# Seven part products for eight in the first sums of the second block's gate and up projections, and attention in two halves of each chunk's tokens

## The chip, the cores and the metric

The kernel runs on one core of a Trainium2 chip. The metric is the device time of one launch in microseconds (us), the median of several runs; less is better.

The core's engines work at once and wait for one another through semaphores: TensorE (PE) multiplies a stationary 128x128 tile of weights, loaded beforehand (PEld), with a moving tile of up to 512 columns and adds the result into a bank of PSUM; VectorE (DVE) and ScalarE (ACT) do elementwise work on SBUF and PSUM; GpSimd (POOL) and SyncE (SP) mainly issue DMA transfers here.

## What is computed

One transformer block over 2048 tokens of width 1024, with all inputs in bf16:

```python
xn = layernorm(x)
q, k, v = split(xn @ wqkv)                 # 32 heads of 32
# each token attends to itself and 7 earlier ones, 2 apart:
logits[s, w] = q[s] . k[s - 2 * w] * 32 ** -0.5      # -1e9 where s - 2 * w < 0
o = sum_w softmax(logits)[s, w] * v[s - 2 * w]
s = o @ wo
g = silu((silu(xn @ w1) * (xn @ w3)) @ w2)  # w1, w3: 1024 x 3584, w2: 3584 x 1024
out = x + s * g
```

## The kernel before

**Tiling.** Two blocks of 1024 tokens, each of two chunks of 512 tokens: chunks 0 and 1, then 2 and 3. Activations lie transposed in SBUF (`xT`: feature on the partitions, tokens along them; its two halves are the two chunks of a block). A block goes through q, k and v, the gate and up projections (14 steps, `up_step(b, fb)`, 256 columns of w1 and w3 each), the down projection (`mlp_down`) and the output projection of attention (`wo`). Attention of a chunk (`attention(c)`) is VectorE work that lies beside those matmuls.

**Seven products for eight.** Each big product is cut into two by two blocks, and 7 block products with sums of blocks take the place of 8 (Strassen's scheme in Winograd's form). In a gate and up step the row blocks are w1 and w3 (so one scheme yields both), and the column blocks the two chunks. The sums of input blocks are made once a block (`xn_sums`, tile `xs`, four sums), the sums of weights once for each of the 14 steps in the first block (`w_sums`: four sums of 128x1024 on VectorE, tile `st`, r8 buffers), stored to `s_dram` and loaded again in the second (`up_load`, 1 MB a step). A step is 56 matmuls of 128x128 by 512 columns: for each i of two tiles of 128 rows, four for each of 7 products. In `up_step` first the gate product `pa` of both i (4 matmuls each), then the product of the first sums, `pe` (`sl(0, i)` by `tx[0]`). Then the tail of the step before is emitted (`flush`), ScalarE copies `pa` to `pb` (`fork`) and `pe` to an SBUF buffer (`us5`), and the other products add on in those banks, with copies, additions (`ua2`, `uh`) and silu on ScalarE and VectorE between them.

The down projection already has one of its products cut once more in this way (`part` in `mlp_down`, L1070): matmuls of 256 columns into quarters of PSUM banks, ScalarE copies between quarters (`dq21`, `dq5`, `dq2`) and VectorE additions (`dq12`, `dq22`). On VectorE the first of `dq22` is the correction that a following part product of the first block adds to.

**Attention of a chunk.** For each of 8 offsets w: two products of q with shifted k (128x2048 each, one for each half of the 8 feature tiles), an addition of the two (2048), two more that halve (1024, 512), the last into `E`. Four DMAs gather `E` into `L`, so that a head's four parts lie side by side; three additions, a maximum over w, subtraction, exponent (ScalarE, L756), sum, reciprocal and product follow, all in 128x1024 f32 or less; four DMAs spread the weights back into `E`. Then for each half of the feature tiles eight products of `E` with shifted v (2048) are added up into `qo`, which `wo` reads.

**What sets the order.** The program is written as a list of operations with what they read and write (`Plan`). TensorE keeps the list's order. For the other engines a planner inside the kernel gives each operation a due time, worked back from TensorE, and lets each engine take the most urgent that is ready, by fixed costs for each kind; the order that comes out is what each engine then runs, strictly one after another. SP's queue issues the loads and half of the gathers, POOL's queue the stores to `s_dram` and `t_dram` and the other half. Load buffers (`r8`) are six of 1 MB; SBUF for attention (`att`) is three of 512 KB; `k2` are eight buffers of 128x512 f32; PSUM has eight banks (`mm`).

All matmuls of `mm(...)` bear line L356, VectorE's two-operand operations L365 (`tt`), ScalarE's copies L370 (`cp`), silu L373, DMAs L379.

Of the kernel before, what the change touches and what calls it, by code (L numbers as in the profile page):

```python
# [244 lines left out]
def kernel(  # L245
# [44 lines left out]
    t_dram = dram.tile([P, FH, 4, CH], FP16, name="t_dram")  # L290
    park = {k: dram.tile([P, NJ, CH], BF16, name=f"park_{k[0]}{k[1]}")
# [10 lines left out]
    E = const.tile([P, NST, W, P], BF16, name="E")  # L302
# [34 lines left out]
    zero = E[:, 0, 0:4, :].rearrange("p w n -> p (w n)")  # L337
# [56 lines left out]
    def xs_cells(i):  # L394
        return [("xs", i, k) for k in range(KH)]
# [305 lines left out]
    def attention(c):  # L701
        u = c % 2
        J4 = [range(0, 4), range(4, 8)]
        r4 = lambda s: s.ap().rearrange("p (j n) -> p j n", j=4)
# [5 lines left out]
        for w in range(W):  # L710
            o = HALO - DIL * w
            pr = []
            for jh in range(2):
                p_t = plan.slot("att", f"p{c}_{w}_{jh}")
                tt(f"qk{c}", mul, lambda p_t=p_t: r4(p_t), lambda jh=jh: qo[:, u, jh * 4:jh * 4 + 4, :],
                   lambda jh=jh, o=o: kT[:, jh * 4:jh * 4 + 4, o:o + CH],
                   qo_cells(u, J4[jh]) + [("k", j) for j in J4[jh]] + ([("k", j, "halo") for j in J4[jh]] if w else []),
                   [p_t], 2048, True)
                pr.append(p_t)
            p0, p1 = pr  # L720
            tt(f"qa{c}", add, lambda p0=p0: r4(p0), lambda p0=p0: r4(p0), lambda p1=p1: r4(p1), [p0, p1], [p0], 2048, True)
            tt(f"qb{c}", add, lambda p0=p0: r4(p0)[:, 0:2], lambda p0=p0: r4(p0)[:, 0:2], lambda p0=p0: r4(p0)[:, 2:4],
               [p0], [p0], 1024, True)
            tt(f"qc{c}", add, lambda w=w: E[:, :, w, :], lambda p0=p0: r4(p0)[:, 0].rearrange("p (q n) -> p q n", n=P),
               lambda p0=p0: r4(p0)[:, 1].rearrange("p (q n) -> p q n", n=P),
               [p0], [("E", w, sq) for sq in range(4)], 512, True)
        if ("v", c) in park:
            halo("v")
            get(c, "v")
        if c == 0:  # L730
            tt("mask", add, lambda: E[:, 0, :, 0:HALO], lambda: E[:, 0, :, 0:HALO], lambda: maskb[:],
               [("E", w, 0) for w in range(W)], [("E", w, 0) for w in range(W)], 128, False)
        plan.lift = SOFT[c]
        L = plan.slot("att", f"L{c}", 2)
        Lv = lambda r: L.ap().rearrange("p (r w n) -> p r w n", r=NR, w=W)[:, r]
        for sq in range(4):
            dma((POOL, SP)[sq % 2], f"L{c}", lambda sq=sq: L.ap()[sq:P:4].rearrange("h (r n) -> h r n", r=NR),
                lambda sq=sq: E[:, sq].rearrange("p w n -> p (w n)"), [("E", w, sq) for w in range(W)], [(L, sq)], 330, 2048)
        zf = lambda s: s.ap().bitcast(FP32)
        z = plan.slot("att", f"z{c}")  # L740
        zv = lambda: zf(z).rearrange("p (w n) -> p w n", w=W)
        LC = [(L, sq) for sq in range(4)]
        tt(f"z{c}", add, zv, lambda: Lv(0), lambda: Lv(1), LC, [z], 1024, False)
        tt(f"z{c}", add, zv, zv, lambda: Lv(2), LC + [z], [z], 1024, False)
        tt(f"z{c}", add, zv, zv, lambda: Lv(3), LC + [z], [z], 1024, False)
        zm = plan.slot("att", f"zm{c}")
        zt = lambda s: zf(s)[:, 0:512].rearrange("p (w n) -> p w n", w=4)

        def tree(t, op):
            tt(f"tr{c}", op, lambda: zt(t), lambda: zv()[:, 0:4], lambda: zv()[:, 4:8], [z], [t], 512, False)  # L750
            tt(f"tr{c}", op, lambda: zt(t)[:, 0:2], lambda: zt(t)[:, 0:2], lambda: zt(t)[:, 2:4], [t], [t], 256, False)
            tt(f"tr{c}", op, lambda: zt(t)[:, 0:1], lambda: zt(t)[:, 0:1], lambda: zt(t)[:, 1:2], [t], [t], 128, False)

        tree(zm, mx)
        tt(f"zd{c}", sub, zv, zv, lambda: zt(zm)[:, 0:1].to_broadcast([P, W, P]), [z, zm], [z], 1024, False)
        plan.op(ACT, f"exp{c}", lambda: nc.scalar.activation(out=zf(z), in_=zf(z), func=ACTF.Exp, scale=scale),  # L756
                [z], [z], 1.07, 0.11, table="exp")
        zs = plan.slot("att", f"zs{c}")
        tree(zs, add)
        plan.op(DVE, f"rec{c}", lambda: nc.vector.reciprocal(out=zt(zs)[:, 0], in_=zt(zs)[:, 0]), [zs], [zs], 0.87)  # L760
        pb = plan.slot("att", f"pb{c}")
        pbv = lambda: pb.ap()[:, 0:1024].rearrange("p (w n) -> p w n", w=W)
        tt(f"pb{c}", mul, pbv, zv, lambda: zt(zs)[:, 0:1].to_broadcast([P, W, P]), [z, zs], [pb], 1024, False)
        for sq in range(4):
            dma((POOL, SP)[sq % 2], f"E{c}", lambda sq=sq: E[:, sq].rearrange("p w n -> p (w n)"),
                lambda sq=sq: pb.ap()[sq:P:4, 0:1024].unsqueeze(1).to_broadcast([32, NR, 1024]),
                [pb], [("E", w, sq) for w in range(W)], 330, 2048)
        plan.lift = 0.0
        for jh in range(2):
            js = slice(jh * 4, jh * 4 + 4)  # L770
            A = lambda js=js: qo[:, u, js, :]
            Ac = qo_cells(u, J4[jh])

            def pv(dst, wr, w, jh=jh, js=js):
                o = HALO - DIL * w
                q4 = lambda a: a.rearrange("p j (q n) -> p j q n", n=P)
                tt(f"pv{c}", mul, lambda: q4(dst()), lambda: E[:, :, w, :].unsqueeze(1).to_broadcast([P, 4, NST, P]),
                   lambda: q4(vT[:, js, o:o + CH]),
                   [("E", w, sq) for sq in range(4)] + [("v", j) for j in J4[jh]]
                   + ([("v", j, "halo") for j in J4[jh]] if w else []), wr, 2048, True)  # L780

            pv(A, Ac, 0)
            B = plan.slot("att", f"B{c}")
            pv(lambda B=B: r4(B), [B], 1)
            tt(f"pa{c}", add, A, A, lambda B=B: r4(B), Ac + [B], Ac, 2048, True)
            for w0 in (2, 4, 6):
                B, C = plan.slot("att", f"B{c}"), plan.slot("att", f"C{c}")
                pv(lambda B=B: r4(B), [B], w0)
                pv(lambda C=C: r4(C), [C], w0 + 1)
                tt(f"pa{c}", add, lambda B=B: r4(B), lambda B=B: r4(B), lambda C=C: r4(C), [B, C], [B], 2048, True)  # L790
                tt(f"pa{c}", add, A, A, lambda B=B: r4(B), Ac + [B], Ac, 2048, True)

# [11 lines left out]
    def xn_sum4():  # L804
        tt("xs3", sub, lambda: xs[:, 3], lambda: xT[:, 0, KH:KT, :], lambda: xs[:, 1], xt_cells(0, 1) + xs_cells(1), xs_cells(3), 2048, True)

# [10 lines left out]
    def up_load(b, fb):  # L817
# [7 lines left out]
        else:  # L825
            dma(SP, f"st.{fb}", lambda: st_v(st), lambda: s_dram[fb], [("sd", fb)], [(st, q) for q in range(4)], 1024, 8192)
            dma(SP, f"w3.{fb}", lambda: wv()[:, 1, KH:KT], lambda: w3_r[:, KH:KT, fc], [], [(wt, 1, 1)], 256, 512)

    def st_v(st):
        return r8v(st, FP16).rearrange("p (q k n) -> p q k n", q=4, k=KH)  # L830

    def w_sums(fb):
# [8 lines left out]
        tt("ws3", sub, sv(3), wv(0, 1), sv(1), Wc(0, 1) + S_(1), S_(3), 1024, True)  # L841
        dma(POOL, "s_dram", lambda: s_dram[fb], lambda: st_v(st), [(st, q) for q in range(4)], [("sd", fb)], 1024, 8192)

    def up_step(b, fb):
# [15 lines left out]
        for i in I:  # L860
            pa.append(bank(f"ua{b}_{fl[i]}"))
            mm(pa[i], wl(0, 0, i), bx[0, 0], True, [(wt, 0, 0)] + xt_cells(0, 0), mark=[("step", b, fb)])
        for i in I:
            pe.append(bank(f"ue{b}_{fl[i]}"))
            mm(pe[i], sl(0, i), tx[0], True, [(st, 0)] + xs_cells(0))
        flush()
        for i in I:
            pb.append(bank(f"ub{b}_{fl[i]}"))
            cp("fork", pb[i].ap, pa[i].ap, [pa[i]], [pb[i]])
        for i in I:  # L870
            sp5.append(plan.slot("k2", "us5"))
            cp("us5", lambda i=i: f32(sp5[i]), pe[i].ap, [pe[i]], [sp5[i]])
        for i in I:
            mm(pa[i], wl(0, 1, i), bx[0, 1], False, [(wt, 0, 1)] + xt_cells(0, 1))
            silu("hA", hv(i, 0), pa[i].ap, [pa[i]], hc(i, 0), 0.48)
# [472 lines left out]
    for b in range(NB):  # L1348
# [19 lines left out]
        else:  # L1368
# [5 lines left out]
            def second():  # L1374
                xn_sum4()
                wk.extend(qkv_load(1))
# [62 lines left out]
```

## Time and profile before

| What | Before |
|---|---|
| Median of 3 runs | 718.12 us (717.82 to 720.67) |
| Profiled execution, its own time | 718.92 us |
| Its span, first to last instruction | 716.9 us |
| TensorE, matmuls | 706.6 us busy, 99% |
| VectorE | 661.9 us busy, 92% |
| ScalarE | 389.4 us busy, 54% |
| Granted TensorE clock | 0.999 |
| DMA | 150.56 MB, 210 GB/s on average |

The profile is of one execution. "Busy" is time with an instruction of the engine in progress; matmuls follow one another so closely that a busy TensorE says little, and its pace is read from the distance between starts. A group's row gives line, engine, operation, out<-in with shapes, the count, busy time, the mean duration in ns and the idle time before. In the chain of work that ended last, each instruction is followed back to what released it. In a list of stretches, each engine's column is its busy time there, with the count in brackets; then come the granted clock, the DMA share and GB/s.

### The profile page before, as it was taken

The page shows a single profiled execution, that of the slowest core. Times are in us where ns is not written, and L with a number is a line of the kernel's source. Part 1 is how long each engine was busy: PE and PEld are TensorE (multiplying, and loading weights), DVE is VectorE, ACT ScalarE, POOL GpSimd, SP SyncE. Part 2 cuts the span into 40 slices and gives each one's busy share as a digit, 9 for nine tenths or more (in the row PEclk, how much of TensorE's full clock was granted, in tenths as well). Part 3 has the DMA queues.
Part 4 walks back from the last instruction along what each step waited for, and adds up shares of the span by engine and source line. Part 5 has one row for each costly group of instructions (what it writes and reads, how often), then busy time and mean ns, then how long its engine had stood idle before and what let it go on. Part 6 is the DMA issues. An engine that isn't in the chain of part 4 may idle for free.

```text
span 716.9 us, 9340 instructions
## 1 busy us (share of the span) xinstructions
PE 706.6 (99%) x3407; PEld 352.3 (49%) x3462; DVE 661.9 (92%) x901; ACT 389.4 (54%) x668; POOL 25.4 (4%) x54
## 2 busy tenths in 40 slices
PE   8999999999999999999999999999999999999997
PEld 5655544444444444744555554444444444455443
DVE  6999999987999999979799999975999997999968
ACT  6755465567565697534535354657565654422233
POOL 0011100100000000000000000000000000000000
PEclk9999999999999999999999999999999999999999
DMA  8579985866544849695554559897537346437523
GB/s 315 214 247 388 370 295 167 283 207 215 183 169 150 305 127 241 144 299 184 192 156 157 176 183 321 267 307 225 194 109 254 113 157 213 155 128 239 177 73 103
DMA packets 127262, 150.56 MB, mean 210 GB/s; under 512 B 12400, under 2 KB 104176, under 8 KB 122864
## 3 DMA queue, kind: packets, MB, share of 16 engines
q1 hardware_dynamic: 113312, 121.58, 52.3%
q0 software_dynamic: 5312, 26.22, 9.3%
q10 hardware_dynamic: 8592, 2.16, 2.2%
q8 instruction: 27, 0.44, 0.3%
q14 instruction: 19, 0.16, 0.1%
HBM read 106.95 MB, written 32.51 MB: 195 GB/s over the span
## 4 chain that ended last, share of the span: by engine, by line
PE 97%; DVE 1%; DMA 1%; issue 1%; SPq 0%; DVEq 0%
PE mm L356 93%; PE mm L1070 3%; DVE r L365 1%; DMA r<-in_A_wqkv_dram 1%; PE mm L508 0%; SPq L379 0%; DVEq L1434 0%; DVEq L365 0%
## 5 line engine op out<-in xcount | busy, mean ns | idle before, releaser
L356 PEld LDWEIGHTS <-r 128*128 128x128 f16 (+1 forms) x2288 | 239.9, 107 | 245.8 <-DMA r<-in_A_wqkv_dram 2.3
L356 PE MATMUL mm<-xs,r 128*128 128x512 f16 x1280 | 295.2, 379 | 0.0
L356 PE MATMUL mm<-xT,r 128*128 128x512 bf16 (+1 forms) x968 | 224.4, 369 | 3.4 <-DMA r<-in_A_wqkv_dram 1.3
L370 ACT COPY k<-mm 128x512 f32<-128x512 f32 (+1 forms) x200 | 115.0, 579 | 87.0 <-PE mm L356 73.0
L356 PE MATMUL mm<-r,h_sb 128*128 128x512 bf16 (+1 forms) x694 | 153.7, 379 | 0.5
L365 DVE TENSOR_TENSOR att<-att 128x2048 bf16<-128x2048 bf16 (+4 forms) x132 | 124.0, 950 | 7.2 <-ACT att L756 5.2
L356 PEld LDWEIGHTS <-h_sb 128*128 128x128 f16 (+1 forms) x800 | 78.2, 98 | 93.2
L370 ACT COPY mm<-mm 128x512 f32<-128x512 f32 (+1 forms) x92 | 51.5, 563 | 81.7 <-PE mm L356 69.5
L365 DVE TENSOR_TENSOR att<-qo,kT 128x2048 bf16<-128x2048 bf16 x64 | 76.8, 1215 | 0.0
L365 DVE TENSOR_TENSOR att<-E,vT 128x2048 bf16<-128x2048 bf16 x56 | 66.2, 1216 | 0.0
L365 DVE TENSOR_TENSOR h_sb<-mm,k 128x512 bf16<-128x512 f32 x96 | 62.8, 680 | 0.9 <-PE mm L356 0.3
L365 DVE TENSOR_TENSOR r<-r,r 128x1024 f16<-128x1024 bf16 (+6 forms) x76 | 58.9, 784 | 1.9 <-DMA r<-in_A_wqkv_dram 1.3
L373 ACT ACTIVATE k<-k 128x512 bf16<-128x512 f32 x56 | 34.7, 630 | 45.1 <-DVE k L365 45.0
L365 DVE TENSOR_TENSOR k<-mm,k 128x512 f32<-128x512 f32 x72 | 47.8, 683 | 9.8 <-PE mm L356 9.5
L365 DVE TENSOR_TENSOR h_sb<-h_sb,k 128x1024 bf16<-128x1024 bf16 x56 | 37.0, 683 | 14.0 <-ACT k L370 14.0
L373 ACT ACTIVATE h_sb<-mm 128x512 bf16<-128x512 f32 x60 | 35.8, 598 | 18.1 <-PE mm L356 18.0
L370 ACT CAST k<-mm 128x512 bf16<-128x512 f32 x56 | 32.5, 587 | 12.4 <-PE mm L356 12.4
L365 DVE TENSOR_TENSOR qo<-qo,att 128x2048 bf16<-128x2048 bf16 x32 | 38.9, 1215 | 0.0
L365 DVE TENSOR_TENSOR h_sb<-h_sb 128x512 f16<-128x512 bf16 (+1 forms) x72 | 37.4, 561 | 1.0 <-DMA h_sb<-in_B_w_dram 0.8
L365 DVE TENSOR_TENSOR r<-r 128x1024 f16<-128x1024 bf16 (+2 forms) x36 | 27.8, 790 | 0.6 <-DMA r<-t_dram 0.6
L356 PE MATMUL mm<-h_sb 128*128 128x512 f16 x96 | 22.4, 379 | 0.1
L373 ACT ACTIVATE xs<-k 128x512 bf16<-128x512 f32 x8 | 5.0, 630 | 20.6 <-DVE k L365 20.6
(98 smaller groups left out, 378.9 us busy)
## 6 DMA issues: line engine op xcount, KB each, us to landing
r<-in_B_w_dram SPq DMA_DIRECT2D x42, 512.0 KB, 4.0
s_dram<-r POOLq DMA_DIRECT2D x14, 1024.0 KB, 5.5
r<-t_dram SPq DMA_DIRECT2D x16, 896.0 KB, 6.6
r<-s_dram SPq DMA_DIRECT2D x14, 1024.0 KB, 4.9
r<-in_A_wqkv_dram SPq DMA_DIRECT2D x11, 1024.0 KB, 6.8
r<-in_B_w_dram SPq DMA_DIRECT2D x12, 896.0 KB, 4.7
h_sb<-in_B_w_dram SPq DMA_DIRECT2D x14, 512.0 KB, 11.2
t_dram<-h_sb POOLq DMA_DIRECT2D x14, 512.0 KB, 6.9
```

Source lines behind the costliest of these rows:

```text
L356: nc.tensor.matmul(cut(ps.ap()), lhsT=lhs[k](), rhs=cut(rhs[k]()), start=(first and k == 0), stop=(last and k == n - 1), skip_group_check= ...
L365: plan.op(DVE, name, lambda: fn(out=o(), in0=a(), in1=b()), rd, wr, occ, 0.08, late=late)
L370: plan.op(ACT, name, lambda: nc.scalar.copy(out=o(), in_=a()), rd, wr, occ, 0.11)
L373: plan.op(ACT, name, lambda: nc.scalar.activation(out=o(), in_=a(), func=ACTF.Silu), rd, wr, occ, 0.11, table="silu")
L1070: nc.tensor.matmul(ps.ap()[:, col * 256:(col + 1) * 256], lhsT=lhs[k](), rhs=r()[:, k, :], start=first and k == 0, stop=False, skip_group_ ...
```

## The change

*The first sums' product in the second block.* `DEEP` holds for block 1: there the product `pe` of the first sums is itself cut in two by two (the weights' rows by i and its four feature tiles in two pairs; the inputs' 512 columns in two halves), and done as 7 part products of two matmuls of 256 columns each for each step, in place of 8 matmuls of 512. They stand in another order: two parts open the step, ahead of the gate product; the others lie between its later products. Three copies of 256 columns on ScalarE (`uq21`, `uq5`, `uq2`) and two additions of 256 columns on VectorE (`uq12`, `uq22`) join the quarters. The four sums of weights that this needs (128x256 each) are made in `w_sums` in the first block, into the part of the weight tile that held w3's first half, and go through a new `u_dram` (256 KB a step, stored by POOL, loaded by SP between w1 and w3's second half). The four sums of inputs (128x512 each, `xn_sums2`) overwrite a part of `xT`; they are made in both blocks, and read in the second.

*Attention.* Every chunk is worked in two halves of 256 tokens: a product covers all 8 feature tiles for 256 tokens (again 128x2048), and the additions after it have half the size and twice the number (1024, 512, 256). `E` is laid out by halves. Gathers and spreads are 8 DMAs of half the size for 4; softmax is done for each half, in 128x512 f32 or less, so there are two exponents for one. Weighted sums have runs of 64 tokens where there were 128.

```diff
+    u_dram = dram.tile([FB, P, 4 * 2 * P], FP16, name="u_dram")
-    E = const.tile([P, NST, W, P], BF16, name="E")
+    E = const.tile([P, 2, 4, W, CH // 8], BF16, name="E")
...
-            for jh in range(2):
-                p_t = plan.slot("att", f"p{c}_{w}_{jh}")
-                tt(f"qk{c}", mul, ... qo[:, u, jh * 4:jh * 4 + 4, :], ... 2048, True)
-            tt(f"qa{c}", add, ... 2048, True)
-            tt(f"qb{c}", add, ... 1024, True)
-            tt(f"qc{c}", add, lambda w=w: E[:, :, w, :], ... 512, True)
+        for h in H2:
+            for w in range(W):
+                tt(f"qk{c}", mul, pj(0, 8), lambda h=h: qo[:, u, :, tok[h]], kw, qc_(h) + kc, [p], 2048, True)
+                tt(f"qa{c}", add, pj(0, 4), pj(0, 4), pj(4, 8), [p], [p], 1024, True)
+                tt(f"qb{c}", add, pj(0, 2), pj(0, 2), pj(2, 4), [p], [p], 512, True)
+                tt(f"qc{c}", add, lambda w=w, h=h: E[:, h, :, w, :], row(0), row(1), [p], ec(h, [w]), 256, True)
...
+    def xn_sums2():
+        tt("xt0", sub, xv(0), xsq(0, 1), xsq(0, 0), xs_cells(0), xv_cells(0), 512, True)
+        tt("xt2", sub, xv(2), xsq(1, 1), xsq(0, 1), xs_cells(0), xv_cells(2), 512, True)
+        tt("xt1", sub, xv(1), xsq(1, 1), xv(0), xs_cells(0) + xv_cells(0), xv_cells(1), 512, True)
+        tt("xt3", sub, xv(3), xsq(1, 0), xv(1), xs_cells(0) + xv_cells(1), xv_cells(3), 512, True)
...
+            dma(SP, f"su.{fb}", lambda: r8v(wt, FP16)[:, 2048:3072], lambda: u_dram[fb], [("ud", fb)], [(wt, 1, 0)], 256, 2048)
...
+        tt("wu0", add, v(0), a(0, 1), a(1, 1), A, U, 256, True)
+        tt("wu1", sub, v(1), v(0), a(0, 0), A + U, U, 256, True)
+        tt("wu2", sub, v(2), a(0, 0), a(0, 1), A, U, 256, True)
+        tt("wu3", sub, v(3), a(1, 0), v(1), A + U, U, 256, True)
+        dma(POOL, "u_dram", lambda: u_dram[fb], lambda: r8v(wt, FP16)[:, 2048:3072], U, [("ud", fb)], 256, 2048)
...
+    DEEP = lambda b, fb: b == 1
...
+        if DEEP(b, fb):
+            pe = [bank(f"ue{b}_{fl[i]}") for i in I]
+            part(0, 0, sr(0, 0), xr_(0, 0), sc + xc, True)
+            part(0, 1, sw(0), xq(0), wc + xv_cells(0))
+            cp("uq21", h2(pe[1], 0), h2(pe[0], 0), [pe[0]], [pe[1]], 0.3)
+            cp("uq5", h2(hs, 0), h2(pe[0], 1), [pe[0]], [(hs, 0)], 0.3)
+            for i in I:
+                pa.append(bank(f"ua{b}_{fl[i]}"))
+                mm(pa[i], wl(0, 0, i), bx[0, 0], True, [(wt, 0, 0)] + xt_cells(0, 0), mark=[("step", b, fb)])
+            part(0, 0, sr(1, 0), xr_(1, 0), sc + xc)
+            part(1, 0, sw(1), xq(1), wc + xv_cells(1))
+            cp("uq2", h2(hs, 1), h2(pe[1], 0), [pe[1]], [(hs, 1)], 0.3)
+            tt("uq12", add, h2(pe[0], 1), h2(pe[0], 1), h2(hs, 1), [pe[0], (hs, 1)], [pe[0]], 256, False)
+            flush()
...
+            c11(0)
+            part(1, 0, sw(2), ..., wc + xv_cells(2))
+            tt("uq22", add, h2(pe[1], 1), h2(pe[1], 0), h2(hs, 0), [pe[1], (hs, 0)], [pe[1]], 256, False)
+            part(0, 1, sw(3), xr_(1, 1), wc + xc)
+            u5(0)
+            c11(1)
+            u2(0)
+            part(1, 0, sr(1, 1), xq(3), sc + xv_cells(3))
+            u5(1)
+            u2(1)
```

Where `part(i, h, ...)` emits two matmuls of 256 columns into half h of the bank `pe[i]`, `c11(i)` is the gate product's second part, `u2(i)` the product of the second sums with its copy `us2`, and `u5(i)` the copy `us5`.

More of the change, by code (lines that the diff above doesn't have):

```diff
@@ L709, in attention @@
             get(c, "k")
-        for w in range(W):
-            o = HALO - DIL * w
-            pr = []
-            for jh in range(2):
-                p_t = plan.slot("att", f"p{c}_{w}_{jh}")
[L715 to L726, printed above, removed]
+        tok = [slice(h * HN, (h + 1) * HN) for h in H2]
@@ L739, in attention @@
[L739 to L747, printed above, removed]
@@ L756, in attention @@
[L756 to L763, printed above, removed]
@@ L764, in attention, with tree @@
[L764 to L767, printed above, removed]
-        plan.lift = 0.0
[L769 to L780, printed above, removed]
+        for h in H2:
+            LC = [(L[h], q) for q in Q4]
+            Lv = lambda r, l=L[h]: (lambda: l.ap().rearrange("p (r w n) -> p r w n", r=NR, w=W)[:, r])
+            zz = plan.slot("att", f"z{c}_{h}")
+            zf = lambda a, b, zz=zz: zz.ap().bitcast(FP32)[:, a:b]
+            zv = lambda zf=zf: zf(0, 512).rearrange("p (w n) -> p w n", w=W)
+            zt = lambda a, b, zf=zf: (lambda: zf(512, 768).rearrange("p (w n) -> p w n", w=4)[:, a:b])
+            tt(f"z{c}", add, zv, Lv(0), Lv(1), LC, [zz], 512, False)
+            tt(f"z{c}", add, zv, zv, Lv(2), LC + [zz], [zz], 512, False)
+            tt(f"z{c}", add, zv, zv, Lv(3), LC + [zz], [zz], 512, False)
+            def tree(op, zz=zz, zv=zv, zt=zt):
+                tt(f"tr{c}", op, zt(0, 4), lambda: zv()[:, 0:4], lambda: zv()[:, 4:8], [zz], [zz], 256, False)
+                tt(f"tr{c}", op, zt(0, 2), zt(0, 2), zt(2, 4), [zz], [zz], 128, False)
+                tt(f"tr{c}", op, zt(0, 1), zt(0, 1), zt(1, 2), [zz], [zz], 64, False)
+            wide = lambda zt=zt: zt(0, 1)().to_broadcast([P, W, HN // 4])
+            tree(mx)
+            tt(f"zd{c}", sub, zv, zv, wide, [zz], [zz], 512, False)
+            plan.op(ACT, f"exp{c}", lambda zf=zf: nc.scalar.activation(out=zf(0, 512), in_=zf(0, 512), func=ACTF.Exp, scale=scale),
+                    [zz], [zz], 0.6, 0.11, table="exp")
+            tree(add)
+            plan.op(DVE, f"rec{c}", lambda zf=zf: nc.vector.reciprocal(out=zf(512, 576), in_=zf(512, 576)), [zz], [zz], 0.47)
+            pbv = lambda zz=zz: zz.ap()[:, 1536:2048]
+            tt(f"pb{c}", mul, lambda pbv=pbv: pbv().rearrange("p (w n) -> p w n", w=W), zv, wide, [zz], [zz], 512, False)
+            for q in Q4:
+                dma((POOL, SP)[q % 2], f"E{c}", lambda q=q, h=h: E[:, h, q].rearrange("p w n -> p (w n)"),
+                    lambda q=q, pbv=pbv: pbv()[q:P:4].unsqueeze(1).to_broadcast([32, NR, 512]),
+                    [zz], ec(h, q=[q]), 165, 1024)
@@ L880, in up_step @@
-        for i in I:
-            mm(pe[i], sl(3, i), bx[1, 1], False, [(st, 3)] + xt_cells(1, 1))
-            tt("ua2", add, lambda i=i: f32(su2[i]), pe[i].ap, lambda i=i: f32(su2[i]), [pe[i], su2[i]], [su2[i]], 512, False)
+        h2 = lambda t, h: (lambda: t.ap()[:, h * 256:(h + 1) * 256])
+        hs = plan.slot("k2", "uhs") if DEEP(b, fb) else None
+        sw = lambda q: [lambda k=k: su_v(wt, q)[:, k, :] for k in range(2)]
+        sr = lambda kh, i: [lambda k=k: st_v(st)[:, 0, 2 * kh + k, i * P:(i + 1) * P] for k in range(2)]
@@ new lines, in up_step, with part, emit @@
+        xr_ = lambda kh, h: [lambda k=k: xs[:, 0, 2 * kh + k, h * 256:(h + 1) * 256] for k in range(2)]
+        xq = lambda q: [lambda k=k: xv(q)()[:, k, :] for k in range(2)]
+        wc, sc, xc = [(wt, 1, 0)], [(st, 0)], xs_cells(0)
+        def part(i, h, lhs, rhs, rd, first=False):
+            ps = pe[i]
+            def emit():
+                for k in range(2):
+                    nc.tensor.matmul(ps.ap()[:, h * 256:(h + 1) * 256], lhsT=lhs[k](), rhs=rhs[k](),
+                                     start=first and k == 0, stop=False, skip_group_check=True)
+            plan.op(PE, "mm " + ps.name, emit, rd, [ps], 2 * 0.1092, 0.0)
```

137 lines of the change are left out of this document (94 added, 43 removed).

## The prediction, made before the result was known

> **What bounds the kernel now.** I read the shares of the page first, then the chain that ended last, then that chain in order of time for one step of the second block, then the timelines of TensorE, VectorE and ScalarE at the places where the change puts something. From the page, the busy times and the chain:
>
> ```profile
> PE 706.6 (99%) x3407; PEld 352.3 (49%) x3462; DVE 661.9 (92%) x901; ACT 389.4 (54%) x668; POOL 25.4 (4%) x54
> ...
> PE 97%; DVE 1%; DMA 1%; issue 1%; SPq 0%; DVEq 0%
> ```
>
> The chain in order of time (start, length, what):
>
> ```profile
> 289.00 3.06 PE mm L1070 x28
> ...
> 527.50 0.05 issue
> 527.56 12.03 PE mm L356 x55
> 539.59 0.05 issue
> ```
>
> TensorE is 97% of the chain and has no stretch without work from 13.3 to 705.5 us. One step of the second block is 56 matmuls of 512 columns; its period is 539.59 - 527.50 = 12.09 us, 0.2158 us each. The down projection already has part products of 256 columns with new weights for each: 28 in 3.06 us, 0.1092 us each. So whatever takes columns off TensorE shortens the run one to one, as long as nothing else is late. VectorE is the one that could be late: 92%, and in stages it has no idle time at all (busy times of each engine by stretch; VectorE is the third):
>
> ```profile
> 62.00:135.00 73.00, 72.69 (x334) 36.29 (x339) 73.00 (x116) 40.41 (x72) 5.82 (x11) 1.00 0.80 281
> 135.00:182.00 47.00, 46.79 (x215) 21.28 (x218) 37.69 (x60) 30.73 (x51) 4.41 (x8) 1.00 0.71 236
> 182.00:300.00 118.00, 117.53 (x576) 57.11 (x584) 116.53 (x145) 81.92 (x137) 2.68 (x5) 1.00 0.61 186
> ```
>
> **The change, part by part.**
>
> *TensorE.* In each of 14 steps of the second block, 8 matmuls of 512 columns become 14 of 256: 112 x 0.2158 = 24.17 us go, 196 x 0.1092 = 21.40 us come: **-2.77 us**. This is all that the change can win. The order of the changed kernel shows the same count (112 fewer and 196 more) and nothing else moved on TensorE but the first sums ahead of the gate products within a step.
>
> [...]
>
> *The first load of the second block.* The sums' weights now stand first in a step, so step 0 needs the tile from s_dram one gate product earlier. Timelines of SP's queue and of TensorE, and the issue's size and time to landing:
>
> ```profile
> 427.17 0.34 SPq L379 DMA_DIRECT2D r<-s_dram  x1
> ```
>
> ```profile
> r<-s_dram SPq DMA_DIRECT2D x1, 1024.0 KB, 6.9
> ```
>
> ```profile
> 433.89 1.89 PE L356 MATMUL mm<-xT,r 128*128 128x512 bf16 x8
> 435.61 1.89 PE L356 MATMUL mm<-xs,r 128*128 128x512 f16 x8
> ```
>
> It lands at 427.17 + 6.9 = 434.1. The old order needs it at 435.6, a margin of 1.5 us; the new one at 433.9. In SP's order the new u_dram load (256 KB) stands ahead of it, behind w1. The 256 KB load issued right behind w1 there landed 0.7 us after it (422.4 + 4.4 against 422.0 + 4.1). The s_dram load is issued only when the last value product frees its buffer, which does not move. So it lands at 434.1 to 434.9, and TensorE waits 0.2 to 1.0 us; both ends widen to 0 (the 256 KB are through before it starts) and 2.2 (another 256 KB like it gets between, and the stores ahead slow it by as much). I take **+0.9 us**, near the measured 0.7 plus the 0.2 already short. Later steps have the margin: the next such load landed 4.8 us before its use, less 1.7 for the order and 1.5 for two u loads.
>
> *VectorE, first block.* Each step adds four sums of 128x256 (row: 282 ns; instructions that do not depend on one another start 0.08 us before the last one's end, as 1215 ns rows that start 1.14 us apart show), some 0.20 to 0.32 each with the waits on one another. From the first weight sums at 73.4 to the first correction on a PSUM quarter at 300.4 I went through VectorE's order, before and after, with these spacings: the weight sums +11.6, chunk 0's logits +4.9 (cutting each pass in halves costs 0.2 us for each of 8 offsets, the rest stood earlier before), its softmax +1.2, chunk 1's logits -3.7 (put off), others -1.9: **+12.1 us**. Idle time by the same reckoning was 12.4 us. So VectorE reaches that place as early as before, with 0.3 us to spare and no pause left. There the trace has:
>
> ```profile
> 300.43 0.76 DVE L365 TENSOR_TENSOR mm<-mm,k 128x256 f32<-128x256 f32 x2
> ...
> 301.03 0.93 PE L1070 MATMUL mm<-r,xs 128*128 128x256 f16 x7
> ```
>
> The first of the two ends at 300.85, 0.2 us before the matmul that follows on it. A pause anywhere in those 227 us, as when the two-half softmax waits for its exponent or the gathers, comes out here: 0 to 1.5 us; I take **+0.3**. With cover gone, each further microsecond of VectorE here is one of TensorE.
>
> *VectorE, second block.* 28 corrections of 128x256 (425 ns, spaced 0.345) are 9.7 us, chunk 2's halves about 3. From 347 to 613 I count +10.3 us against 18.7 idle. Within a step the additions have about 2 us: between the product whose copy feeds one and the product that needs its result lie 8 + 4 matmuls of 0.2158 and two of 0.1092 = 2.81 us, less a copy of 0.37 and the addition's 0.42. One 1.14 us instruction ahead in the queue fits, two (2.28) do not by 0.3; the order shows two only at the third step. **0**, up to 0.3 for each of a few steps.
>
> *ScalarE.* Three copies of 256 columns (0.36) a step, off the path: 8 matmuls of 512, 1.73 us, cover the first two. Each exponent is now in two, each with a table load before and after; the order has 22 loads for 14. The timeline of ScalarE at the first exponent before:
>
> ```profile
> 159.69 1.28 ACT L756 ACT_TABLE_LOAD   x1
> 160.99 1.06 ACT L756 ACTIVATE att<-att 128x1024 f32<-128x1024 f32 x1
> ```
>
> Behind the second exponent of chunk 2 stand the two quarter copies that step 5's third part needs: 1.28 + about 0.6 + 0.36 + 0.37 = 2.6 us of ScalarE against 1.73 of cover plus what it runs ahead. I take **+0.2** (0 to 0.9). [...] The trace shows the exponent 0.02 us after the load's end and the load 0.01 after the copy before it.
>
> *DMA.* u_dram adds 14 stores and 14 loads of 256 KB; the up steps have 0.5 to 0.6 DMA share, and the load goes where a half of w3 was not loaded. The gathers double in number at half size. 0, except at step 0. *The first block's extra input sums* (4 x 0.33) have no reader there; they are in the count. *The tail* after 705.5 is untouched.
>
> Sum: -2.77 + 0.9 + 0.3 + 0.2 = **-1.4 us**. Against the profiled execution's own 718.92 (span 716.9 and 2.0 around it) that is 717.5. Its median of runs is 718.12, 0.8 lower, so I forecast **716.7 us**. No change that can be told is 0.5%, 3.6 us: 714.5 to 721.7.
>
> **The rivals.**
>
> *All covered.* The load at step 0 is in time and nothing waits: 718.12 - 2.77 = 715.4. For it: TensorE's order is otherwise without gaps, and margins elsewhere are 1 us and more. Against: the 434.1 against 433.9.
>
> *VectorE becomes the bound (slower).* No row has bf16 operands in runs of 64 elements, which the weighted sums of a chunk now read, or stores of 64; the 128-long and 512-long runs of the trace take the same 1215 ns. If the 32 long instructions of a chunk cost 10% more, that is 32 x 0.114 = 3.6 us in the stretch to 300 where 0.3 us is left, and again for chunk 1, as VectorE is idle for 0.03 us from 347 to 468. With the forecast's -1.4 that gives 718.12 - 1.4 + 3.6 to 7.2 = 720.3 to 723.9, likeliest 722. It decides from 4% on, where 1.4 us are eaten up. For it: 92% now and some 97% after. Against it: halves and quarters of other tiles run at the rate of whole ones in the trace (128x1792 in pieces of 128 takes 1081 ns, on the same line as 128x2048).
>
> [...]
>
> **How the numbers follow.** The forecast (waits of 0.5 to 2.5 us in all, 715.8 to 718) 0.57; all covered, 0.2; VectorE as the bound 0.14 (of it 0.08 above 721.7); waits of 2.5 to 4 without it, 718 to 719.5, 0.08; parts at full price 0.01. The range leaves out the upper half of the slow rival: **714.8 to 720.5**. Faster by over 0.5% would need more than the columns give, 0.04; slower 0.09; within 0.87.
>
> **What would show it.** Right: a step's period in the second block of 11.89 us; the s_dram load of step 0 landing after the gate product could have begun, with a gap of near 1 us on TensorE at 433 to 435; VectorE without a pause from 65 to 300 and a wait for it near 301. Wrong: instructions with runs of 64 above 1215 ns; a period above 11.9, which would be the additions or copies in the seams; gaps on TensorE at the exponents above 1 us.

## The result, and the profile after

The changed kernel takes **741.5 us** (median of 6 runs, 739.8 to 745.1) against 718.1 us before (median of 6, 717.5 to 720.7). The ratio is 1.032, 95% interval 1.029 to 1.035: slower by 3.2%, where 716.7 us and no measurable difference were forecast. The profiled execution took 741.81 us, its span is 740.0 us, its mean granted clock 0.993.

The page of the changed kernel, busy times and chain:

```profile
PE 712.3 (96%) x3490; PEld 361.3 (49%) x3546; DVE 692.9 (94%) x1137; ACT 401.5 (54%) x722; POOL 41.9 (6%) x84
...
PE 23%; DVE 6%; issue 1%; DMA 1%; ACT 0%; DVEq 0%; POOL 0%; ACTq 0%; POOLq 0%
```

This chain could be followed back from its end only to 510.5 us, where it meets a spread of chunk 2 (`E<-att`, below), so its shares add up to 31%: TensorE has 23 of these and VectorE 6, where VectorE had 1% of the whole chain before. TensorE's busy share went from 99% to 96%; it does fewer columns in *more* busy time, 712.3 us for 706.6. VectorE has 31 us more work, 692.9 for 661.9. What the engines wait for is in the lists of waits of the changed kernel (engine, tile, line, what it waited for: us in total, times, longest), first TensorE's, then VectorE's, then ScalarE's:

```profile
PE mm L907 <- ACT k L371: 8.4, 2, 5.6
...
PE mm L907 <- DMA r<-s_dram: 0.6, 1, 0.6
```

```profile
DVE att L366 <- DMA E<-att: 11.3, 4, 3.2
DVE att L366 <- DMA att<-E: 5.0, 2, 4.2
DVE att L768 <- DMA E<-att: 3.4, 1, 3.4
```

```profile
ACT L765 <- DMA E<-att: 6.0, 1, 6.0
```

The second and third lists are the finding. `E<-att` are the spreads of the softmax weights from an attention buffer back to `E`, `att<-E` the gathers into it. Operations *on the attention buffers* (`att`) wait for spreads, and so does a table load on ScalarE: 11.3 + 3.4 + 6.0 = 20.7 us in four chunks, and 5.0 us for gathers. The lists of before have a single wait on an attention DMA:

```profile
DVE att L365 <- DMA att<-E: 1.4, 1, 1.4
```

The spreads of a half only read that half's buffer; nothing in the other half's softmax needs them.

One place shows how such a wait reaches TensorE. ScalarE, then VectorE twice, then TensorE, by start (start, length, what; in brackets the idle time before and what ended it), chunk 2 of the changed kernel:

```profile
513.75 1.28 ACT L765 ACT_TABLE_LOAD   x1 [6.00 <-DMA E<-att]
515.04 0.63 ACT L765 ACTIVATE att<-att 128x512 f32<-128x512 f32 x1
515.58 0.37 ACT L371 COPY mm<-mm 128x256 f32<-128x256 f32 x1
515.88 0.36 ACT L371 COPY k<-mm 128x256 f32<-128x256 f32 x1
```

```profile
494.37 0.69 DVE L366 TENSOR_TENSOR att<-att 128x512 f32<-128x512 bf16 x1 [4.18 <-DMA att<-E]
...
509.52 0.69 DVE L366 TENSOR_TENSOR att<-att 128x512 f32<-128x512 f32 x1 [2.79 <-DMA E<-att]
```

```profile
516.30 0.59 PE L907 MATMUL mm<-xs,r 128*128 128x256 f16 x2 [5.61 <-ACT k L371]
```

The first line of VectorE is the first addition of the first half's softmax. By the landing times in the trace the first half's four gathers were in by 486.7 us; the addition starts at 494.4, when the second half's are in too (492.6 to 494.1). VectorE's subtraction for the second half (509.52) and the second half's exponent with its table load (513.75) stand still until the first half's spreads have landed (three by 509.4 us; the fourth, which POOL's queue held back until that subtraction, at 513.6). Behind the exponent in ScalarE's queue stand the two quarter copies that a step of the gate/up product needs (515.58 and 515.88), and TensorE is idle for 5.6 us. Then it also runs at a granted clock of 0.50, and eight matmuls of 512 columns take 3.62 us (from 517.10), where eight take 1.89 before the gap (from 508.80). TensorE's busy time, granted clock, DMA share, GB/s by stretch:

```profile
508.00:514.00 6.00, 2.69 (x15) 1.00 0.78 236
516.00:518.00 2.00, 1.70 (x7) 0.50 0.00 0
522.00:524.00 2.00, 2.00 (x13) 1.00 0.76 291
```

So this gap is charged twice: 5.6 us as idle time, and once more as slow matmuls behind it. That is part of why the busy time of TensorE grew.

### The profile page after: what moved, and what is told of

Same layout as the page of the kernel before. It is cut to its first block, busy times and chain, and to the rows that moved or that the text cites. A ratio compares the mean times of both kernels' runs of the same rounds, so it can differ in the third digit from the quotient of the medians.

```text
span 740.0 us, 9890 instructions
## 1 busy us (share of the span) xinstructions
PE 712.3 (96%) x3490; PEld 361.3 (49%) x3546; DVE 692.9 (94%) x1137; ACT 401.5 (54%) x722; POOL 41.9 (6%) x84
## 5 line engine op out<-in xcount | busy, mean ns | idle before, releaser
L357 PEld LDWEIGHTS <-r 128*128 128x128 bf16 (+1 forms) x2176 | 229.7, 108 | 230.2 <-issue 12.2
L357 PE MATMUL mm<-xs,r 128*128 128x512 f16 x1168 | 277.8, 382 | 4.7 <-DVE h_sb L366 2.0
L357 PE MATMUL mm<-xT,r 128*128 128x512 bf16 (+1 forms) x968 | 227.1, 369 | 2.7 <-DMA r<-in_A_wqkv_dram 0.4
L371 ACT COPY k<-mm 128x512 f32<-128x512 f32 (+1 forms) x228 | 122.3, 556 | 60.6 <-PE mm L357 47.6
L366 DVE TENSOR_TENSOR att<-att 128x1024 bf16<-128x1024 bf16 (+8 forms) x240 | 134.7, 592 | 20.0 <-DMA E<-att 11.3
L371 ACT COPY mm<-mm 128x512 f32<-128x512 f32 (+1 forms) x106 | 55.7, 535 | 77.9 <-DVE h_sb L366 25.6
L366 DVE TENSOR_TENSOR r<-r,r 128x1024 f16<-128x1024 bf16 (+7 forms) x104 | 66.7, 651 | 1.8 <-DMA r<-in_A_wqkv_dram 1.6
L371 ACT CAST k<-mm 128x512 bf16<-128x512 f32 x56 | 32.6, 591 | 11.3 <-PE mm L357 10.9
L366 DVE TENSOR_TENSOR r<-r 128x1024 f16<-128x1024 bf16 (+2 forms) x64 | 35.9, 573 | 0.0
L907 PEld LDWEIGHTS <-r 128*128 128x128 f16 x196 | 19.2, 98 | 24.5 <-issue 9.9
L380 POOL DMA_DIRECT2D att<-E x16 | 8.8, 557 | 326.3 <-DVE E L366 326.3
```

The source lines that it names most:

```text
L357: nc.tensor.matmul(cut(ps.ap()), lhsT=lhs[k](), rhs=cut(rhs[k]()), start=(first and k == 0), stop=(last and k == n - 1), skip_group_check= ...
L366: plan.op(DVE, name, lambda: fn(out=o(), in0=a(), in1=b()), rd, wr, occ, 0.08, late=late)
L371: plan.op(ACT, name, lambda: nc.scalar.copy(out=o(), in_=a()), rd, wr, occ, 0.11)
L380: plan.op(eng, name, lambda: e.dma_start(out=o(), in_=a()), rd, wr, occ, 0.0, nbytes=kb * 1024, late=late, run=run)
L907: nc.tensor.matmul(ps.ap()[:, h * 256:(h + 1) * 256], lhsT=lhs[k](), rhs=rhs[k](), start=first and k == 0, stop=False, skip_group_check=True)
```

## The experiments

**Theory A** comes from the waits of the instructions in the trace. The three attention buffers are slices of *one* tile (`plan.wide`). The kernel's own planner, which orders the instructions, takes them for three independent buffers. The program built from that order does not: operations on one slice hold waits for DMAs on another. In the changed kernel the first addition of a chunk's softmax waits for up to 8 DMAs (in chunks 1 and 2), where its own half has 4 gathers, and the table load of an exponent waits for up to 13. With one softmax a chunk there is no other half to wait for. (The DMAs address every fourth partition, `[q:P:4]`; that this is why the slices are not kept apart is argued, not tried.) **Rival B** is the added work: 31 us more on VectorE, part products, more copies.

*First four kernels: the two parts of the change, and the buffer.* `sep` is the changed kernel with three tiles in place of one. `halves` is before with the attention in halves alone, `halves_sep` the same with three tiles. `deep` is before with the part products alone, attention by whole chunks.

```diff
-        "att": [None] * 3,
+        "att": [const.tile([P, 4 * CH], BF16, name=f"att_{i}") for i in range(3)],
...
-    plan.wide = {"att": (const.tile([P, 12 * CH], BF16, name="att"), 4 * CH)}
```

Expected of `sep`:

> The changed kernel with the three attention buffers as three tiles instead of slices of one; instructions and their order per engine stay, only the waits differ. Theory A (shared tile: the second half's softmax waits for the first half's gathers and spreads, though it touches other buffers): the waits of VectorE and ScalarE on spreads (20.7 us in all) go, TensorE's gaps go, 715.5 to 718 us. Rival B (VectorE has too much work, and the part products' copies and additions leave seams): waits move to other places, 735 to 741 us.

Expected of `halves`:

> The kernel before with attention in halves alone, buffers in one tile; no part products. Theory A: the waits are in these halves, VectorE has some 24 us less to do and hides a part of them: 722 to 735 us. Rival B: VectorE has room for the halves' 15 us (677 of 717), so within 2 us of the kernel before.

Expected of `halves_sep`:

> As halves, with three tiles. Theory A: 717 to 719 us, no waits on spreads. Rival B: the same as halves, whatever that is.

Expected of `deep`:

> The kernel before with the part products alone, attention in whole chunks as before. Theory A: the columns' -2.77 us less the waits at the first step of the second block (about 0.9) and near 300 us: 715.5 to 718 us. Rival B: the work that the parts add to VectorE (24 us) and the seams cost: 725 us or more.

| Kernel | Median, us | Ratio to before (95%) | Span | TensorE busy | VectorE busy |
|---|---|---|---|---|---|
| changed | 741.5 | 1.032 (1.029 to 1.035) | 740.0 | 712.3 | 692.9 |
| `sep` | 720.5 | 1.003 (1.002 to 1.004) | 718.1 | 705.1 | 692.6 |
| `halves` | 742.8 | 1.034 (1.032 to 1.035) | 740.3 | 711.8 | 670.9 |
| `halves_sep` | 719.8 | 1.001 (1.000 to 1.002) | 717.8 | 706.6 | 671.8 |
| `deep` | 742.9 | 1.034 (1.031 to 1.036) | 742.8 | 712.8 | 685.1 |

Three tiles for one take back 741.5 - 720.5 = 21.0 us of the changed kernel, and 742.8 - 719.8 = 23.0 us of the halves alone. The order of the instructions is the same in both of a pair, on every engine; only the tile names and the waits differ. VectorE's work is the same too (692.9 and 692.6). So the cause of the changed kernel's loss is theory A's, and what is left for B is what `sep` keeps over before, 2.0 of 23 us. No VectorE or ScalarE wait on an attention DMA is left in `sep`'s lists. Of the 21.9 us by which the spans differ, 14.7 us are idle time of TensorE and 712.3 - 705.1 = 7.2 us busy time. The clock explains 4.2 of these: in the changed kernel 3.4 + 4.9 = 8.3 us of matmuls ran at a granted clock of 0.50, in `sep` none, and at that clock eight of 512 columns took about twice as long (3.41 us between starts, 517.10 to 520.51, for 1.73 in `sep`, 509.59 to 511.32). The other 3.0 are in line with the edges of the gaps: the last matmul before a gap counts as busy for 0.38 us, where in a row the next one starts after 0.22. By an estimate from these two rows that is 0.16 us for each of some 17 more gaps, 2.7 us. Theory A mis-sized all three: `sep` is 2.5 us above its upper end, `halves_sep` 0.8 above, and `halves` lost 7.8 more than its upper end.

`deep` broke theory A as a complete account. It has no halves and one softmax a chunk, and before, with the same shared tile, has just the one wait of 1.4 us; yet `deep` loses as much. Its list of TensorE's waits names VectorE:

```profile
PE mm L357 <- DVE h_sb L366: 10.2, 4, 6.1
PE mm L357 <- DVE r L366: 4.3, 1, 4.3
```

**Theory C**, formed on this: the sums of weights put some 12 us more on VectorE in the first block; a whole softmax has stretches that VectorE cannot fill; so it comes late to what lies behind, the weight sums that TensorE needs near 381 to 385 us and the last chunk's attention. **Rival D**: the loss in `deep` lies in the buffer or in TensorE.

*`deep_lite`: `deep` without that work.* It leaves out the four weight sums of each first-block step and stores other finite sums in their place, so the second block's gate/up values are not the reference's.

```diff
-        tt("wu0", add, v(0), a(0, 1), a(1, 1), A, U, 256, True)
-        tt("wu1", sub, v(1), v(0), a(0, 0), A + U, U, 256, True)
-        tt("wu2", sub, v(2), a(0, 0), a(0, 1), A, U, 256, True)
-        tt("wu3", sub, v(3), a(1, 0), v(1), A + U, U, 256, True)
-        dma(POOL, "u_dram", lambda: u_dram[fb], lambda: r8v(wt, FP16)[:, 2048:3072], U, [("ud", fb)], 256, 2048)
+        dma(POOL, "u_dram", lambda: u_dram[fb], lambda: st_v(st)[:, 0].rearrange("p k n -> p (k n)"), A, [("ud", fb)], 256, 2048)
```

> The part products alone with the whole-chunk softmax of before, as in the run deep (742.9), but the first block's four weight sums a step are left out (56 VectorE operations, 12.1 us of work; the second block reads other finite sums in their place, so the gate/up values of the second block are not the reference's). Theory C (in deep, VectorE has idle time in each whole softmax, carries the added sums behind it and delivers the down weights' sums and the last chunk's attention late): the two gaps near 358 and 385 us (7.4 us, and the slow clock behind them) shrink to under 1.5 us and the time falls to 716-728. Rival D (the loss lies in the shared attention buffer or in TensorE itself, not in VectorE's load): within 3 us of deep, 738-746.

Measured: 717.6 us, ratio 0.999 (0.998 to 1.000). VectorE has 13.3 us less work (685.1 to 671.8), the time is 25.3 us shorter, and both gaps near 358 and 385 us are gone. That speaks for C and against D. But the planner orders `deep_lite` anew as well: besides the 56 sums that are gone, some 400 of VectorE's other 937 operations stand elsewhere when the two traces are lined up. So how much of the 25.3 us is the work, and how much the order that came with it, was not separated. VectorE by stretch (length, busy time with count, granted clock, DMA share, GB/s), before, `sep`, `deep` and `deep_lite` from 65 to 340 us:

```profile
65.00:340.00 275.00, 259.14 (x360) 1.00 0.71 226
```

```profile
65.00:340.00 275.00, 271.66 (x480) 1.00 0.74 238
```

```profile
65.00:340.00 275.00, 265.16 (x413) 1.00 0.73 236
```

```profile
65.00:340.00 275.00, 259.70 (x366) 1.00 0.73 238
```

The idle 275.0 - 259.1 = 15.9 us of before is where the forecast's 12.1 us were to go. `sep` fills all but 3.3 of it. `deep` leaves 9.8 idle, puts in only 6.0 us more, and the rest comes after 340 us, where VectorE had next to no room before (0.03 us idle from 347 to 468). By these rows the two halves do have a use: they give VectorE something to do while one of them is with the DMAs or ScalarE. Whether part of `deep`'s own loss is the shared tile was not tried; it has one wait of 4.2 us on a gather at 343 us.

*Edits on `sep`.* `sep` is still 2 us above before, although its TensorE has 2.8 us less to do. Its waits of TensorE, and ScalarE at the first of them:

```profile
PE mm L906 <- DMA r<-s_dram: 1.3, 1, 1.3
PE mm L356 <- ACT mm L370: 1.3, 1, 1.3
```

```profile
339.86 1.28 ACT L373 ACT_TABLE_LOAD   x1
341.15 0.60 ACT L373 ACTIVATE h_sb<-mm 128x512 bf16<-128x512 f32 x1
341.77 1.28 ACT L764 ACT_TABLE_LOAD   x1
343.06 0.63 ACT L764 ACTIVATE att<-att 128x512 f32<-128x512 f32 x1
343.60 1.06 ACT L370 COPY mm<-mm 128x512 f32<-128x512 f32 x2
```

One activation stands between the two halves' exponents and costs two table loads, 2.6 us of ScalarE; the copies that TensorE needs wait behind them. The other wait is the first load of the second block. `sep_gate` runs the gate products of that step ahead of its parts again:

```diff
         if DEEP(b, fb):
+            if not fb:
+                for i in I:
+                    pa.append(bank(f"ua{b}_{fl[i]}"))
+                    mm(pa[i], wl(0, 0, i), bx[0, 0], True, ...)
             pe = [bank(f"ue{b}_{fl[i]}") for i in I]
             part(0, 0, sr(0, 0), xr_(0, 0), sc + xc, True)
...
-            for i in I:
-                pa.append(bank(f"ua{b}_{fl[i]}"))
-                mm(pa[i], wl(0, 0, i), bx[0, 0], True, ...)
+            if fb:
+                for i in I:
+                    pa.append(bank(f"ua{b}_{fl[i]}"))
+                    mm(pa[i], wl(0, 0, i), bx[0, 0], True, ...)
```

> The changed kernel with three attention buffers of their own (run sep, 720.5), and in the second block's first step alone the two gate products run ahead of the parts. Theory: the 1.5 us gap of sep at 437.8 us is the wait for the step's first load, which comes 1.9 us later into the step this way: the gap goes, 719.0 (718.5 to 719.6). Rival (the load is late by whatever asks for it, and the wait moves along, or the later order costs elsewhere): 720.0 to 721.0.

`sep_exp` makes each exponent wait for both halves:

```diff
             tt(f"zd{c}", sub, zv, zv, wide, [zz], [zz], 512, False)
+            soft.append((zz, zf, zv, wide, tree))
+        for h in H2:
+            zz, zf, zv, wide, tree = soft[h]
             plan.op(ACT, f"exp{c}", ...
-                    [zz], [zz], 0.6, 0.11, table="exp")
+                    [soft[0][0], soft[1][0]], [zz], 0.6, 0.11, table="exp")
```

> The changed kernel with three attention buffers of their own (run sep, 720.5), and the two halves' exponents made to follow each other, each waiting for both halves, so that the table is loaded 18 times and not 22. Theory: sep's gap of 1.4 us near 344 us is ScalarE's reloading between a half's exponent, a sigmoid-like activation and the other half's exponent; it goes, 718.6 to 719.6. Rival (the later exponent of the first half holds VectorE's softmax up, which then is idle): same or slower, 720.3 to 722.

`sep_best` has both, and not the first block's input sums, which nothing reads:

```diff
             xn_sums()
-            xn_sums2()
```

> Both edits of sep_gate and sep_exp together, and without the four sums of normalized inputs in the first block, which nothing reads there. Theory: the gaps of sep (3.4 us) go, and what is left is the 2.8 us that the smaller products save, less up to 1: 716.0 to 717.5, faster than before (718.1) by 0.1 to 0.3%. Rival (VectorE, at 97% of the span, gives back what ScalarE and the loads free): 718.5 to 720.5.

Measured: `sep_gate` **727.5** us (1.012, 1.011 to 1.014), `sep_exp` **736.6** (1.026, 1.024 to 1.027), `sep_best` **736.4** (1.025, 1.023 to 1.027). None came out as the theory said; they are 7 to 16 us worse than `sep`. TensorE's waits in `sep_exp`:

```profile
PE mm L356 <- DVE h_sb L365: 7.9, 4, 3.0
PE mm L356 <- DVE r L365: 5.1, 1, 5.1
```

The same two results of VectorE are late as in `deep`. The rival of `sep_exp` named the mechanism, not the size (it said 720.3 to 722): VectorE now waits 5.1 us on exponents in all, 0.2 in `sep`. But each edit also makes the planner order all engines anew, so these runs alone cannot tell the edit from the order.

*`sep_swap`: the edit without the new order.* It takes `sep`'s planned order and moves only the two gate products of that step on TensorE. TensorE's order is then that of `sep_gate`, and the other four engines' that of `sep`.

```diff
-        for o in self.simulate():
+        order = self.simulate()
+        gate = [o for o in order if o.name in ("mm ua1_0", "mm ua1_1")][:2]
+        first = next(o for o in order if o.name == "mm ue1_0")
+        i = order.index(first)
...
+        for o in gate:
+            order.remove(o)
+        order[i:i] = gate
+        for o in order:
             o.emit()
```

> Run sep (720.5) with the two gate products of the second block's first step ahead of its parts on TensorE, as in sep_gate (727.5), but with every other engine's order kept as in sep: TensorE's order is sep_gate's, that of the other four is sep's. Theory F (sep_gate's extra 7 us came with VectorE's and ScalarE's newly planned order, not with the two products that changed place): the gap at 437.8 us shrinks from 1.5 to under 0.6 us and the time is 719 to 720.6. Rival (the changed place itself costs it): 725 to 729.

Measured: 719.9 us (1.002, 1.001 to 1.003), in theory F's range. So the 7.6 us between `sep_gate` and `sep_swap` are the new order of the other engines alone: VectorE's, ScalarE's and that of ten issues in SP's queue (POOL's is the same in both traces). Against `sep` (1.003, 1.002 to 1.004) the edit by itself gains nothing that can be told. The wait for the load is gone, but the gap shrank only to 0.79 us, more than F's 0.6: TensorE now waits there for a copy of ScalarE.

*GpSimd for VectorE.* `deep_pool`, `sep_pool` and `sep_pool_all` do the four weight sums on GpSimd, which is idle 94 to 96% of the time in `sep` and `deep`; `deep_pool` and `sep_pool_all` also lack the unread sums, and `sep_pool_all` has the edits of `sep_best`.

```diff
-        tt("wu0", add, v(0), a(0, 1), a(1, 1), A, U, 256, True)
+        gt("wu0", nc.gpsimd.tensor_add, v(0), a(0, 1), a(1, 1), A, U, 0.6)
...
+    def gt(name, fn, o, a, b, rd, wr, occ):
+        plan.op(POOL, name, lambda: fn(out=o(), in0=a(), in1=b()), rd, wr, occ, 0.1)
```

> The part products alone, whole-chunk softmax, as in deep (742.9); the four weight sums of each step of the first block are done by GpSimd, which is 4% busy, and the four sums of normalized inputs that nothing reads in the first block are gone. Theory C (deep loses because VectorE's 12.1 us more of first-block work makes everything behind it late): VectorE's load is that of deep_lite, so the time is near its 717.5: 716.5 to 719. Rival E (GpSimd's sums slow VectorE's operations down while they run, or come too late for the step's weights to be released): gaps of TensorE in 65 to 290 us, or VectorE's 128x2048 operations above 1217 ns on the mean, 722 to 740.

> Run sep (720.5) with the four weight sums a step of the first block on GpSimd. Theory C: sep has no gap that VectorE alone causes, so relief of VectorE gives little: the gaps near 344 us (table loads) and 438 us (first load) stay, 718 to 721. Rival E as in deep_pool: 724 to 745.

> sep_best (736.4: gate products first in the first step, exponents next to each other, no unread sums) with the four weight sums a step of the first block on GpSimd. Theory C: what sep_best lost was VectorE coming late to the sums that TensorE waits for at 381 us and to the last attention; with 12.1 us less to do in front of them both waits go, and the savings of the edits show: 716 to 718.5. Rival (the later first exponent alone sets when the softmax ends): still above 725.

Measured: `deep_pool` 725.8 us (1.010, 1.007 to 1.012), `sep_pool` 730.6 (1.018, 1.016 to 1.019), `sep_pool_all` 740.5 (1.031, 1.029 to 1.032). All three came out in their rivals' ranges. `deep_pool` is 17 us better than `deep`, as C wants, and 8 worse than `deep_lite`, which is rival E's; these orders, too, are planned anew, and where `deep_pool` loses the 8 us was not traced. For `sep_pool` GpSimd's rows show where time goes: here one sum and the gathers issued behind it and its successors, then the VectorE addition that waited for these gathers, and the matmul that waited in the end:

```profile
140.34 7.49 POOL L368 TENSOR_TENSOR r<-r 128x256 f16<-128x256 f16 x1
...
152.23 1.12 POOL L382 DMA_DIRECT2D att<-E  x2
```

```profile
157.87 0.69 DVE L365 TENSOR_TENSOR att<-att 128x512 f32<-128x512 bf16 x1 [6.56 <-DMA att<-E]
```

```profile
163.92 3.57 PE L356 MATMUL mm<-xs,r 128*128 128x512 f16 x8 [6.50 <-ACT k L373]
```

A sum that takes 0.66 us at best took 7.49. GpSimd's queue also issues half of the attention's gathers; SP's queue issued its two for the same half of chunk 0 at 140.6 us, GpSimd's went out at 152.2 and landed by 157.7. VectorE waited 6.6 us, the exponent behind it, and TensorE 6.5. No version that does the whole computation beat the kernel before.

## Why the prediction was wrong

- **The step that failed** is the *DMA* part of the working: "The gathers double in number at half size. 0, except at step 0." It counted the DMAs and their bytes, and not who waits for them; the one place where it allowed for such a wait is the first block's VectorE term, with 0 to 1.5 us. The working took over the planner's view that the two halves are independent, but they are slices of one tile, and in the built program one half's softmax waits for the other half's DMAs (20.7 us on spreads alone). Measured by three tiles for one, that step is 21.0 us, more than the range allowed for everything. One of the prediction's own signs of being wrong came: gaps on TensorE at the exponents above 1 us (2.0 us at 348, 5.6 at 516).
- *TensorE -2.77 us*: right. In `sep`, two first parts of steps that follow each other:

```profile
449.67 0.38 PE L906 MATMUL mm<-xs,r 128*128 128x256 f16 x2
...
461.56 0.38 PE L906 MATMUL mm<-xs,r 128*128 128x256 f16 x2
```

  461.56 - 449.67 = 11.89 us, the forecast period. No run shows the forecast's case of parts at full price (0.01): the page of the changed kernel has 196 loads of the parts' weights of 0.098 us, 14 a step; by an estimate from this row, a step that paid for each would take 11.89 + 14 x 0.098 = 13.26 us.

```profile
L907 PEld LDWEIGHTS <-r 128*128 128x128 f16 x196 | 19.2, 98 | 24.5 <-issue 9.9
```

- *First load of the second block, +0.9*: right in kind and size. The changed kernel waits 0.6 us for it, `sep` 1.3, within the 0 to 2.2.
- *VectorE, first block, +0.3*: right where the buffers are separate. In `sep` VectorE does 271.7 - 259.1 = 12.5 us more between 65 and 340 us (the forecast was 12.1 from 73 to 300 us), and at 301.6 us TensorE waits 0.2 us for the correction that the prediction named:

```profile
PE mm L1166 <- DVE mm L365: 0.2, 1, 0.2
```

  But the working said that "each further microsecond of VectorE here is one of TensorE", and then gave pauses only 0 to 1.5 us. In `deep` 13.3 us of VectorE work, with the order that came with them, went with 25.3 us of time.
- *ScalarE, table loads, +0.2 (0 to 0.9)*: too small even in `sep`. Between 340 and 348 us the matmuls of `sep` fall 1.9 us further behind the same matmuls of before, at the place with the 1.3 us wait for ScalarE's copies. The count of 22 loads was right, what stood behind them was looked at for one chunk only (chunk 2; the place is chunk 1's). The table load itself cost its 1.28 us and no more: the second exponent starts at 343.06 us, 0.01 us after the load from 341.77 ends.
- *Rival "VectorE becomes the bound"*: its mechanism, runs of 64 elements, did not come. The group of the changed kernel's weighted sums takes what it took before, 1216 ns:

```profile
L366 DVE TENSOR_TENSOR att<-E,vT 128x2048 bf16<-128x2048 bf16 x56 | 66.6, 1217 | 0.0
```

  That its sign was right is luck: the changed kernel is slower for its waits, not for slow instructions. The rival was given 0.08 above 721.7 us, and 741.5 lay outside every case. VectorE did move onto the path: it has 19% of the chain that ended last in `sep`, 1% before.
- *What is left in `sep`*: it should gain 2.8 us and loses 2.0 by the medians, 718.1 - 716.9 = 1.2 by the spans of the profiled executions. Where these 1.2 arise shows when the starts of the same matmuls are compared in the traces of before and `sep`. `sep` is 0.4 us ahead at first; it loses 0.5 at 168 us behind a copy of ScalarE, 0.1 near 252, 0.3 at 301 and 1.9 between 340 and 348. The second block gives back only 1.2: the 2.77 less the 1.34 of the first load and some 0.2 at places without a listed wait. So with separate tiles the mis-sized term is ScalarE's: some 2.4 us for the forecast 0.2. The 0.8 us by which the medians differ more than the profiled executions stay open.

## What to carry to other kernels

When a change cuts one sequence into two that are meant to overlap, look at the waits in the built program, not at the plan: two buffers that are slices of one tile can be one buffer to it, and a DMA on one slice then holds up the other (21 to 23 us here, with not one instruction moved). An engine as busy as VectorE here (92% of the span before, 96% in `sep`), with a fixed order, had no price per microsecond: 13 us of VectorE work, with the order that came with them, went with 25 us of time, and a new order of the same work alone with 7.6. To learn what an edit costs where a planner reorders everything, keep the planned order and move only the instructions in question.

## What the runs showed of the hardware

- Half clock after a gap. In the changed kernel the granted clock is 0.50 from within the 5.6 us gap (0.81 from 514 to 515 us, 0.50 from 515 to 516) until about 521 us. After the 2.8 us gap that ends at 496.95 us it is 1.00 from 497.0 to 497.5 us, 0.55 from 497.5 to 498 and 0.50 from 498 to 500, so it fell some 0.6 us after work had begun again. After a gap of 2.8 us in `deep`, which ends at 358.74 us, four matmuls of 512 columns took 1.09 us and the next eight 3.56, where eight take 1.89 from 353.11 us. After the 2.0 us gap at 348 us of the changed kernel and the 1.25 us gap at 344 us of `sep` it stays 1.00.
- GpSimd beside a busy VectorE. The first sums of a pair took 0.66 to 8.27 us for the same 128x256 (median 0.69) in `sep_pool`, and 0.66 to 7.89 (median 0.99) in `deep_pool`. All 56 of `deep_pool` took 77.5 us of GpSimd; on VectorE, in `deep`, the same 56 are rows of 0.28 us, 15.7 us. Two of the long ones, beside VectorE: the sum shown above ends at 147.83 us, 0.6 us after VectorE had begun an operation that reads PSUM (`k<-mm,k` at 147.22). In `deep_pool` a sum from 103.38 us took 7.67 and ends at 111.05, again 0.6 us after VectorE had begun such an operation (`k<-mm,k` at 110.44); from 103.75 to 110.44 us VectorE began eight operations, all with their inputs in SBUF. Why the sums end there is not shown by these runs. VectorE's own long operations were only 2% slower (1236 ns for 1215, in `deep_pool`).
